# Seven quarter products for half of a feed-forward's first part, in idle score banks, and attention weights turned in place

## The chip, the cores and the metric

The kernel runs on one core of a Trainium2 chip. Its time is device time in microseconds (us); before the change it is 1347.37 us, the median of three runs (1346.15 to 1348.08). The engines are TensorE (PE in the profile; PEld is its weight loads), VectorE (DVE), ScalarE (ACT), GpSimd (POOL) and SyncE (SP, which only issues transfers here). Everything is float32.

## The reference

Attention with a threshold is followed by a normalised feed-forward block with a residual.

```python
# q, k, v: (8, 8, 576, 64): batch, heads, sequence, head size
scores = q @ k^T / 8
thresh = max(scores, -1) - tau                  # tau = 0.02
scores = where(scores >= thresh, scores, -1e9)
attn   = exp(scores - max) ; attn /= sum(attn) + 1e-9
x      = (attn @ v), heads side by side         # (8, 576, 512)
xn     = (x - mean) / sqrt(var + 1e-6) * g_ln
out    = x + relu(xn @ w_ch1) @ w_ch2           # w_ch1 512 x 2048, w_ch2 2048 x 512
```

## The kernel before

The main loop has 72 slots (`n`), nine for each of the 8 batches. A slot is one block of attention: two heads and half of the queries, or (the fifth of nine, `s == HP`) the last 32 queries of each half for all heads. In a slot

- PE computes the scores of the block into two PSUM areas, `sc[0]` and `sc[1]` (three banks each; the first 128 columns of each are free, `FREE`), named sc in the profile;
- DVE takes the row maxima (L419), ACT copies the finished values of an earlier block out (L621) and computes the exponentials into `e` (L432), DVE applies the threshold and sums the rows (L439, the masks), POOL divides (L455), and DVE turns `e` in 32 x 32 blocks into another tile, `et` (L529, or L523 for the fifth block); in between DVE turns new q and k (`turn`, L356 to L366) in slots that load them;
- SP stores `et` to a scratch tensor in DRAM (L540, scr<-et) and reloads it in the layout that PE needs (L554, em<-scr and L559, er<-scr);
- a slot later PE multiplies these turned weights by v (`values_of`, L598 sc<-em and L608 sc<-er, the value products), into the last columns of the score areas (`pv_behind`).

From slot 7 on all slots have one `e` tile, since `exponentials` picks `e_room[0]` for them.

The feed-forward works on 16 groups `g` of 288 tokens, two in each batch, numbered in the order in which they come ready. Its steps are a generator (`ffn_steps`), and `second_part` takes some of them in each of a slot's four quarters, by shares (`ROOM`): quarters 0 to 2 lie between the scores and the value products, quarter 3 between these and the rest of the value products (L608). So the order on every engine is fixed when the program is built, and each engine goes through its own list in order. A step that has no place in a quarter waits for the next one; nothing is put in its place while the chip runs.

- The first part (`first_part`) computes 16 tiles `p` of hidden units: four products of 128 x 128 weights with 288 tokens each, in one PSUM bank (two banks, `ps_ff`, are used in turn), and ACT's Relu (L796) takes each tile out. `product` splits each into two instructions of 64 columns of weights; a float32 instruction is two records in the profile. Beside it the variance is computed: Square on ACT (L802), three adds on POOL (L804), a product, three steps on ACT (L816 to L818), and `root` on DVE (L737 to L741).
- The second part (`second_quarters`, L101 seg in the profile) is already computed by seven quarter products in place of eight, with sums and differences by DVE and POOL (L872 and L912).

Where `drip`, `drops`, `aside` and `stores` appear, they are lists of small calls that are put among the rest of a slot.

Of the kernel before, what the change touches and what calls it, by code (L numbers as in the profile page):

```python
# [18 lines left out]
def kernel(  # L19
# [70 lines left out]
    hidden = consts.tile([128, ND, TOK], F32, name="hidden")  # L90
    e_room = [consts.tile([128, 4, S], F32, name=f"e{i}") for i in range(2)]

    units = [(b, hp) for b in range(B) for hp in range(HP)]
# [83 lines left out]
    class Weights:  # L177
# [13 lines left out]
        def __init__(self):  # L191
# [17 lines left out]
            self.raw, self.ticks = {}, 2  # L209
            flat = lambda t: t.rearrange("p a b -> p (a b)")  # L210

            x_room = ffn.tile([128, NK, TOK], F32, tag="x", bufs=3, name="x_room")
            y_room = ffn.tile([128, NK, TOK], F32, tag="sq", bufs=1, name="y_room")
            et_room = att.tile([128, NB, 128], F32, tag="et", bufs=1, name="et_room")
            stage = self.stage = consts.tile([128, 8, WC], F32, name="stage")
# [6 lines left out]
            for t, n, before in (  # L222
                (w2_sb.rearrange("p m d c -> p (m d) c"), ND // 2, lambda p: (16, 16, 19, 21, 24, 24, 25, 29)[p]),
                (hidden, 4, lambda p: 10),
                (x_room, 1, lambda p: 2 * n1),
                (y_room, 1, lambda p: 2 * n1),
                (et_room, 2, lambda p: n1 - 3),
                (stage, 4, lambda p: 2 * n1),
            ):
                for p in range(n):  # L230
                    home = 99 if t.shape[-1] != 128 or n != ND // 2 else n1 + 2 * p
                    self.free.append(
                        (before(p), -1, flat(t)[:, p * 2 * WC : (p + 1) * 2 * WC], home)
                    )
# [94 lines left out]
    FIRST = HP + 2  # L329

    def by_blocks(n):

        return n >= FIRST

    def scale_q(u, q_in):
# [75 lines left out]
    def exponentials(n):  # L411
# [17 lines left out]
        for i in range(4):  # L429
            if i == 2:  # L430
                yield es, thr
            nc.scalar.activation(es[:, i], blocks[i], func=AF.Exp, bias=neg[:, i : i + 1])  # L432

    def weights(es, thr, divide):


        den = small.tile([128, 4], F32, tag="den", name="den")
        for i in range(4):
            nc.vector.scalar_tensor_tensor(  # L439
                out=es[:, i], in0=blocks[i], scalar=thr[:, i : i + 1], in1=es[:, i],  # L440
                op0=ALU.is_ge, op1=ALU.mult, accum_out=den[:, i : i + 1],
            )
            if divide and i % 2:
                nc.vector.reciprocal(den[:, i - 1 : i + 1], den[:, i - 1 : i + 1])  # L444
# [3 lines left out]
        for i in range(4):  # L448
            if not divide:
                if i % 2 == 0:  # L450
                    two = ffn.tile([128, TOK], F32, tag="o", bufs=4, name="diag")
                diags.append(two[:, i % 2 * 128 : i % 2 * 128 + 128])
                nc.scalar.mul(diags[i], ident, den[:, i : i + 1])
                continue
            nc.gpsimd.tensor_scalar(  # L455
                out=es[:, i], in0=es[:, i], scalar1=den[:, i : i + 1], scalar2=1.0,
                op0=ALU.mult, op1=ALU.mult,
# [60 lines left out]
    def turn_blocks(b, s, es):  # L518


        et = att.tile([128, NB, 128], F32, tag="et", bufs=1, name="et")
        if s == HP:
            nc.vector.transpose(  # L523
                et.rearrange("p n (u c) -> p u n c", u=HP),
                es.rearrange("p u (n c) -> p u n c", c=32),
            )
        else:
            for h in range(2):
                nc.vector.transpose(  # L529
                    et[:, :, 64 * h : 64 * h + 64].rearrange("p n (j c) -> p j n c", j=2),  # L530
                    es[:, 2 * h : 2 * h + 2].rearrange("p j (n c) -> p j n c", c=32),
                )
        scr = dram.tile([4, S, 128], F32, tag="scr", name="scr")
        if b == 0:
# [219 lines left out]
    def differences():  # L754
# [9 lines left out]
        for eng, out, a, b, op in (  # L764
# [5 lines left out]
            for m in range(HM):  # L770
                for d in range(0, HD, 4):
                    at = (slice(None), m, slice(d, d + 4))
                    eng.tensor_tensor(out=out[at], in0=a[at], in1=b[at], op=op)
                    yield

    def first_part(g):

# [5 lines left out]
        for d in range(ND):  # L783
# [15 lines left out]
            if sq is None and d and (part > 1 or d == ND // 2 - 1):  # L799
                squared = d  # L800
                sq = hidden[:, ND - NK :]
                nc.scalar.activation(sq, xc, func=AF.Square)  # L802
                for c in range(1, NK):
                    nc.gpsimd.tensor_tensor(out=sq[:, 0], in0=sq[:, 0], in1=sq[:, c], op=ALU.add)  # L804
            elif sq is not None and rb is None and (
                d >= squared + (7 if plain else 3) and part > (0 if plain else 1)
                or d == ND - NK - 1
            ):
                var = ps_ff.tile([128, TOK], F32, tag="ff", name="var")
                product(var, lhsT=avg_sb, rhs=sq[:, 0], start=True, stop=True)  # L810
                rb = ffn.tile([128, TOK], F32, tag="rb", bufs=2, name="rb")
                two = [sq[:, c] for c in (2, 3)]
                if plain:
                    two = [ffn.tile([128, HM, HT], F32, tag="part", bufs=4, name="two") for _ in two]
                    two = [t.rearrange("p m t -> p (m t)") for t in two]
                nc.scalar.activation(two[0], var, func=AF.Identity, bias=eps_sb)  # L816
                nc.scalar.activation(rb, two[0], func=AF.Ln)
                nc.scalar.activation(rb, rb, func=AF.Exp, scale=-0.5)  # L818
                aside.append(lambda: root(rb, *two))
                yield 1, 1  # L820
# [21 lines left out]
    def second_quarters(g, rb):  # L842
# [68 lines left out]
        def add(eng, out, a, b):  # L911
            eng.tensor_tensor(out=out, in0=a, in1=b, op=ALU.add)  # L912

        def finish(eng, i, j=None):

# [52 lines left out]
        if not ends_here:  # L968
            later(
                ("12", 1, add, dve, y12, y12, p3), ("done12", 2, finish, pool, 0, 1),  # L970
                *((f"o{m}", 1, store, dve, g, m, y[:, m]) for m in (2, 3, 0, 1)),
            )
        yield 2, 0.5

    def ffn_steps(g):
        rb = yield from first_part(g)
        yield from (second_quarters if g else second_plain)(g, rb)

# [5 lines left out]
    ROOM = (0.6, 1.0, 1.25, 0.35)  # L984
    STEPS = [1 + NK * ND * 2] + [1 + NK * ND * 2 - NK * ND // 8] * (NG - 1)
    ends = [sum(STEPS[: i + 1]) for i in range(NG)]
# [19 lines left out]
    def second_part(n, i):  # L1006
# [11 lines left out]
        steps = 0  # L1018
        got = 1 if i in (0, QUARTERS - 1) else 2
        while queue and (owed >= 0.5 or got == 1 and i in (0, QUARTERS - 1)):  # L1020
            got, cost = next(queue[0], (None, 0))
# [6 lines left out]
            else:  # L1028
                issued += cost
                owed -= cost  # L1030
                steps += 1
                if steps == 4 and among:
                    mean_of(among[0])
                    centre(among.pop())

    def group_ready(g):
# [4 lines left out]
        else:  # L1041
            at_quarter(*before, mean_of, g)
            at_quarter(*(first if g and first[1] else before), centre, g)
        at_quarter(*first, lambda: queue.append(ffn_steps(g)))

# [43 lines left out]
    for n in range(NS):  # L1089
# [45 lines left out]
        blocks_go = by_blocks(n)  # L1135
        diags = weights(es, thr, blocks_go)
        run_all(aside)
# [9 lines left out]
        if blocks_go:  # L1147
            conversion.fetch(0 if n == FIRST + 2 else 3, wait=0)
            conversion.prepare_to(end_at, False)
            scr = turn_blocks(b, s, es)  # L1150
            if n == FIRST:
                conversion.take(e_room[1])
# [84 lines left out]
```

## Time and profile before

| what | value |
|---|---|
| median of the runs | 1347.37 us |
| span of the profiled execution | 1345.5 us |
| busy PE | 1313.5 us, 98% |
| busy DVE, POOL, ACT | 870.6, 621.9, 458.7 us (65%, 46%, 34%) |
| DMA, mean over the span | 159 GB/s |
| steady slots (from slot 18 on) | 15.4 to 19.9 us each, nine together 158.4 us |
| after the last scores (slot 71 starts 1231.9 us after the first instruction) | 113.6 us |

The median of the runs is taken outside the profiler; the span of the profiled execution, from its first to its last instruction, lies 1.9 us under the median. Busy time of matmuls counts each record, and the records overlap: a record of 288 columns lasts 408 ns by itself, but the next one starts after about 122. In a row of a group the columns are: line, engine, operation, output and inputs with their sizes, count, then busy time and mean duration, and last the idle time just before them with what ended it. In a timeline the columns are start and duration in us.

### The profile page before, as it was taken

The numbers are of one execution on the slowest core, as the hardware profiler recorded it, in microseconds if no ns is written. First come the engines' busy times: TensorE is split into PE (matmuls) and PEld (weight loads), VectorE is DVE, ScalarE is ACT, GpSimd is POOL, SyncE is SP. The second block draws the span as 40 slices with busy tenths as digits, with TensorE's granted clock in tenths as the row PEclk, the third lists the DMA queues.
The fourth block names the chain that finished last, engine by engine and source line by source line (L and its number), as shares of the span: only waits on it lengthen the run. The fifth ranks groups of instructions, "written<-read, shape, count | busy, mean of one in ns | idle before, by whom it ended". The sixth has DMA issues, their size and how long they took to land.

```text
span 1345.5 us, 40255 instructions
## 1 busy us (share of the span) xinstructions
PE 1313.5 (98%) x17304; PEld 989.7 (74%) x17304; DVE 870.6 (65%) x1544; ACT 458.7 (34%) x995; POOL 621.9 (46%) x836
## 2 busy tenths in 40 slices
PE   8898899999999999999999999999999999999997
PEld 7665567769686776868778696877869677786957
DVE  7879886667666675666756677656756667666112
ACT  5866333232323233232233324233232323333120
POOL 3475556534444444445535454443444445335312
PEclk9999999999999999999999999999999999999999
DMA  8937874557643775447734576447754476443211
GB/s 173 297 95 176 209 191 151 178 163 190 176 146 132 182 200 158 151 156 200 191 127 150 167 183 191 139 137 196 198 167 152 126 196 179 136 157 124 81 19 20
DMA packets 335298, 213.92 MB, mean 159 GB/s; under 512 B 247376, under 2 KB 292688, under 8 KB 327056
## 3 DMA queue, kind: packets, MB, share of 16 engines
q1 hardware_dynamic: 329008, 210.46, 54.6%
q8 instruction: 136, 2.23, 0.7%
q10 hardware_dynamic: 5952, 0.74, 0.4%
q0 software_dynamic: 160, 0.15, 0.1%
q14 instruction: 42, 0.34, 0.1%
HBM read 124.00 MB, written 87.29 MB: 157 GB/s over the span
## 4 chain that ended last, share of the span: by engine, by line
PE 91%; ACT 3%; DVE 2%; DMA 1%; POOL 1%; issue 1%; SPq 1%; POOLq 0%; ACTq 0%; DVEq 0%
PE p L101 38%; PE seg L101 31%; PE sc L405 10%; PE sc L598 9%; PE sc L608 2%; ACT e L432 1%; PE tp L101 1%; DVE e L439 1%; POOL w L308 1%; PE var L101 1%; PE mean L101 1%; SPq L118 0%; DMA scr<-et 0%; ACT em L489 0%; DMA k_in<-in_k_dram 0%
## 5 line engine op out<-in xcount | busy, mean ns | idle before, releaser
L101 PE MATMUL p<-xc,w 128*64 128x288 f32 x4096 | 517.1, 408 | 6.5 <-ACT part L887 4.6
L101 PEld LDWEIGHTS p<-xc,w 128*64 128x64 f32 x4096 | 287.7, 137 | 213.8 <-issue 13.5
L419 DVE TENSOR_REDUCE neg<-sc 128x2 f32<-128x1152 f32 x144 | 188.7, 1351 | 282.2 <-PE sc L405 281.6
L455 POOL TENSOR_SCALAR e<-e,den 128x576 f32<-128x576 f32 x264 | 205.9, 792 | 131.3 <-DVE den L444 131.3
L101 PE MATMUL seg<-hidden,w 128*64 128x144 f32 x3840 | 247.9, 287 | 0.0
L101 PEld LDWEIGHTS seg<-hidden,w 128*64 128x64 f32 x3840 | 234.9, 137 | 11.5 <-issue 8.5
L439 DVE SCALAR_TENSOR_TENSOR e<-sc,thr,e 128x576 f32<-128x576 f32 x288 | 222.4, 810 | 19.3 <-POOL thr L423 11.6
L423 POOL TENSOR_SCALAR thr<-neg,low_sb 128x2 f32<-128x2 f32 x144 | 39.4, 274 | 384.1 <-DVE neg L419 382.4
L796 ACT ACTIVATE hidden<-p 128x288 f32<-128x288 f32 x256 | 106.5, 416 | 305.3 <-PE p L101 303.7
L432 ACT ACTIVATE e<-sc,neg 128x576 f32<-128x576 f32 x288 | 197.6, 754 | 2.4 <-DVE neg L419 2.4
L529 DVE STREAM_TRANSPOSE et<-e 128x1152 f32<-128x1152 f32 x118 | 161.1, 1373 | 14.2 <-POOL e L455 13.7
L405 PE MATMUL sc<-kT,qT 64*64 64x384 f32 (+3 forms) x2048 | 140.3, 403 | 3.1 <-DVE e L439 3.1
L598 PE MATMUL sc<-em,v_in 128*64 128x128 f32 (+1 forms) x2368 | 130.9, 264 | 2.4 <-DVE w L293 2.4
L598 PEld LDWEIGHTS sc<-em,v_in 128*64 128x64 f32 x2368 | 124.0, 138 | 10.9 <-DVE w L293 2.6
L101 PE MATMUL seg<-hidden,stage 128*64 128x144 f32 x1920 | 123.3, 286 | 0.0
L101 PEld LDWEIGHTS seg<-hidden,stage 128*64 128x64 f32 x1920 | 117.6, 137 | 2.9 <-issue 2.9
L621 ACT COPY x<-sc 128x128 f32<-128x128 f32 x120 | 31.6, 265 | 245.2 <-PE sc L405 176.3
L405 PEld LDWEIGHTS sc<-kT,qT 64*64 64x64 f32 x2048 | 76.3, 133 | 44.6 <-issue 21.3
L872 POOL TENSOR_TENSOR hidden<-hidden 128x576 f32<-128x576 f32 x60 | 84.8, 1427 | 52.0 <-ACT hidden L796 42.4
L887 ACT COPY part<-seg 128x288 f32<-128x288 f32 x74 | 29.8, 403 | 190.6 <-PE seg L101 190.1
L872 DVE TENSOR_TENSOR hidden<-hidden 128x576 f32<-128x576 f32 x60 | 51.2, 887 | 51.5 <-PE seg L101 48.5
L101 PE MATMUL seg<-hidden,e 128*64 128x144 f32 x896 | 61.2, 286 | 0.0
(130 smaller groups left out, 1041.2 us busy)
## 6 DMA issues: line engine op xcount, KB each, us to landing
scr<-et SPq DMA_DIRECT2D x63, 1152.0 KB, 4.8
em<-scr SPq DMA_DIRECT2D x63, 1024.0 KB, 5.7
out_dram<-ot SPq DMA_DIRECT2D x248, 36.0 KB, 3.8
q_in<-in_q_dram SPq DMA_DIRECT2D x120, 72.0 KB, 2.7
er<-scr SPq DMA_DIRECT2D x132, 64.0 KB, 5.2
k_in<-in_k_dram SPq DMA_DIRECT2D x116, 72.0 KB, 3.0
v_in<-in_v_dram SPq DMA_DIRECT2D x28, 256.0 KB, 5.4
w<-in_moe_w_ch_dram SPq DMA_DIRECT2D x10, 512.0 KB, 7.0
```

Source lines behind the costliest of these rows:

```text
L101: nc.tensor.matmul(out[r], lhsT=lhsT[:, r], rhs=rhs, **flags)
L405: nc.tensor.matmul(sc[h][64 * i : 64 * i + 64, at : at + n], lhsT=ql[r] if s == HP else qT[r, half, j * 128 + 64 * i : j * 128 + 64 * i + 64],
L419: nc.vector.tensor_reduce(out=neg[:, i], in_=pairs[h], axis=AXL.X, op=ALU.max, negate=True,)
L423: nc.gpsimd.tensor_scalar(out=thr[:, i], in0=neg[:, i], scalar1=-1.0, scalar2=low_sb, op0=ALU.mult, op1=ALU.add,)
L432: nc.scalar.activation(es[:, i], blocks[i], func=AF.Exp, bias=neg[:, i : i + 1])
L439: nc.vector.scalar_tensor_tensor(out=es[:, i], in0=blocks[i], scalar=thr[:, i : i + 1], in1=es[:, i], op0=ALU.is_ge, op1=ALU.mult, accum_o ...
L455: nc.gpsimd.tensor_scalar(out=es[:, i], in0=es[:, i], scalar1=den[:, i : i + 1], scalar2=1.0, op0=ALU.mult, op1=ALU.mult,)
L529: nc.vector.transpose(et[:, :, 64 * h : 64 * h + 64].rearrange("p n (j c) -> p j n c", j=2), es[:, 2 * h : 2 * h + 2].rearrange("p j (n c) ...
L598: nc.tensor.matmul(dst[64 * h : 64 * h + 64], lhsT=vt[:, h, c, :], rhs=pick(em[:, 2 * j : 2 * j + 2, c], h), start=c == 0 and first, stop= ...
L621: nc.scalar.copy(x_of(2 * b + (s > HP))[:, s % (HP + 1), 128 * j : 128 * j + 128], pv[j])
L796: nc.scalar.activation(hidden[:, d], p1, func=AF.Relu)
L872: eng.tensor_tensor(out=out[at], in0=in0[at], in1=in1[at], op=op)
```

## The change

In the first part of groups 2 to 15, 8 of the 16 tiles are no longer computed one by one. They form two units of four tiles (0 to 3 and 12 to 15). A unit is a 2 x 2 block product: two halves of the hidden units, two halves of the input features, and two halves of the tokens (`early`, `late`), with seven products of quarters in place of eight. Five of the seven go into the banks of `ps_ff`, four of them one upon another in `chain`, which ACT copies out three times on the way; two go into the free first columns of the banks 0 and 1 of `sc[0]`, in the second half of a slot, after the masks have read the scores. DVE adds the parts (`sums_due`), and ACT takes the Relu in place.

The units need sums of the weights (`sums_of_w1`, made once during group 1) and of the tokens (`sum_x`, four subtractions in each group). The sums of weights lie in a new tile `extra`, with the last three pieces in `e_room[1]` and `ident`; up to slot 11 `extra` also serves as `et`, which is gone: from slot 12 on the weights of attention are turned within `e` itself, which for that is written in another order (`blocks_of`), and SP stores them from there. The variance of a group is computed after the first unit, and its Square at the start of that unit; before, both came at a count of tiles. A unit may start in a slot's third quarter of the slots in `unit_slots`, or as soon as no plain tile is left; a step that ends with 4 ends the quarter.

```diff
+    IN_PLACE = SLOTS + HP - 1
+    def blocks_of(es, i, n):
+        if n < IN_PLACE:
+            return es[:, i]
+        return flat(es).rearrange("p (n u c) -> p u n c", u=4, c=32)[:, i]
...
     def turn_blocks(b, s, es):
-        et = att.tile([128, NB, 128], F32, tag="et", bufs=1, name="et")
+        if b * SLOTS + s >= IN_PLACE:
+            et = flat(es).rearrange("p (n x) -> p n x", x=128)
+            for at in (slice(0, 128),) if s == HP else (slice(0, 64), slice(64, 128)):
+                nc.vector.transpose(et[:, :, at], et[:, :, at])
...
+    UNITS = (((0, 1), (2, 3)), ((12, 13), (14, 15)))
...
+    def sums_of_w1():
+        for k, (f1, f2) in enumerate(UNITS):
...
+                    for eng, out, a, b, op in (
+                        (nc.gpsimd, p3, a11, a21, ALU.subtract),
+                        (nc.vector, a21, a21, a22, ALU.add),
+                        (nc.vector, p2, a21, a11, ALU.subtract),
+                        (nc.gpsimd, p4, a12, p2, ALU.subtract),
+                    ):
+                        eng.tensor_tensor(out=out, in0=a, in1=b, op=op)
...
+    def sum_x(g):
+        while g - 1 not in last_added:
+            drops.pop(0)[-1]()
...
+        for eng, out, a, b in (
+            (nc.vector, t1, b12, b11), (nc.gpsimd, t3, b22, b12),
+            (nc.vector, t2, b22, t1), (nc.gpsimd, t4, b21, t2),
+        ):
+            eng.tensor_tensor(out=out, in0=a, in1=b, op=ALU.subtract)
...
+    def unit(g, xc, k):
...
+        chain = ps_ff.tile([128, 2, HT], F32, tag="ff", name="chain")
+        for _ in steps(chain, w_of(f1, 0), x_of(0, 0), True, False):
+            yield 3, 0.5
+        nc.scalar.copy(h12, chain)
+        p2 = ps_ff.tile([128, 2, HT], F32, tag="ff", name="p2")
+        for _ in steps(p2, w_of(f1, 1), x_of(1, 0), True, True):
+            yield 3, 0.5
+        add = lambda out, a, b: nc.vector.tensor_tensor(out=out, in0=a, in1=b, op=ALU.add)
+        sums_due.append(lambda: add(h11, p2, h12))
+        for end in steps(chain, s_of(0), t_of(t2), False, False):
+            yield 4 if end and part < 2 and now < QUARTERS * NS else 3, 0.5
+        nc.scalar.copy(h22, chain)
+        for _ in steps(other[0], w_of(f2, 0), t_of(t1), True, True):
+            yield 3, 0.5
+        sums_due.append(lambda: add(h12, other[0], h22))
+        for _ in steps(chain, s_of(1), t_of(t3), False, False):
+            yield 3, 0.5
+        nc.scalar.copy(h21, chain)
+        sums_due.append(lambda: add(h22, other[0], h21))
+        for end in steps(other[1], s_of(2), x_of(1, 1), True, True):
+            yield 4 if end and now < QUARTERS * NS else 3, 0.5
+        sums_due.append(lambda: add(h12, other[1], h12))
+        for end in steps(chain, w_of(f2, 1), t_of(t4), False, True):
+            if not end:
+                yield 3, 0.5
+        run_all(sums_due)
+        nc.scalar.activation(h21, chain, func=AF.Relu)
+        both = hidden[:, f1[0] : f1[0] + 2]
+        nc.scalar.activation(both, both, func=AF.Relu)
+        nc.scalar.activation(h22, h22, func=AF.Relu)
+        yield 2 if k else 3, 0.5
...
+    def first_units(g):
...
+            if k < len(UNITS) and (not plain or now // QUARTERS >= slots[k] and part > 1):
+                if g not in sums_of_x:
+                    sum_x(g)
+                if k == 0:
+                    squares(sq, xc)
+                yield from unit(g, xc, k)
+                k += 1
+                if k == 1:
+                    rb = variance(sq, [sq[:, c] for c in (2, 3)])
+                    yield 2, 1
+                continue
...
     def ffn_steps(g):
-        rb = yield from first_part(g)
-        yield from (second_quarters if g else second_plain)(g, rb)
+        rb = yield from (first_part if g < 2 else first_units)(g)
+        sums = sums_of_w1() if g == 1 else iter(())
+        for i, step in enumerate((second_quarters if g else second_plain)(g, rb)):
+            if i % 8 == 7:
+                next(sums, None)
+            yield step
...
-        got = 1 if i in (0, QUARTERS - 1) else 2
-        while queue and (owed >= 0.5 or got == 1 and i in (0, QUARTERS - 1)):
+        has_unit = g > 1 and n in unit_slots(g)
+        whole = i in (0, QUARTERS - 1) or i == 1 and has_unit
+        got = 1 if i in (0, QUARTERS - 1) else 3 if i == 2 and has_unit else 2
+        while queue and (owed >= 0.5 or got == 3 or got == 1 and whole):
...
+                if got == 4:
+                    break
...
             scr = turn_blocks(b, s, es)
+            run_all(sums_due)
```

## Prediction

> **What bounds the kernel now.** I read the page first (engines, then the costliest groups), then the trace slot by slot: the timeline of all engines for slots 16 to 21, then the windows. A slot is one pass of the main loop: scores of one block, its softmax, the value products of the block before, and a share of the feed-forward work.
>
> ```profile
> span 1345.5 us, 40255 instructions
> PE 1313.5 (98%) x17304; PEld 989.7 (74%) x17304; DVE 870.6 (65%) x1544; ACT 458.7 (34%) x995; POOL 621.9 (46%) x836
> ...
> L101 PE MATMUL p<-xc,w 128*64 128x288 f32 x4096 | 517.1, 408 | 6.5 <-ACT part L887 4.6
> ...
> L101 PE MATMUL seg<-hidden,w 128*64 128x144 f32 x3840 | 247.9, 287 | 0.0
> ```
>
> TensorE (PE) is busy 98%. The windows say where the other 2% lies: slots 16, 17 and 20 whole, then a stretch around a wait early in the run (columns: length, then busy time of PE, PEld, DVE, ACT, POOL, then the granted clock).
>
> ```profile
> 264.77:281.36 16.59, 16.57 (x181) 10.10 (x177) 11.61 (x21) 6.70 (x16) 7.75 (x10) 1.00 0.43 148
> 281.36:298.19 16.83, 16.83 (x192) 10.91 (x188) 10.14 (x18) 5.56 (x13) 6.94 (x10) 1.00 0.70 185
> 333.72:351.52 17.80, 17.80 (x193) 11.01 (x188) 11.56 (x22) 6.94 (x15) 10.07 (x13) 1.00 0.77 221
> 154.21:157.90 3.69, 3.69 (x30) 2.99 (x32) 3.59 (x8) 1.95 (x3) 3.69 (x5) 0.57 1.09 250
> ```
>
> In the steady slots PE has no gap at all: whatever PE does less is gained, and whatever it waits more is lost, one for one. The other engines are at 60% or less there, but each slot's softmax is one long chain. The timeline of slot 17 (start, duration):
>
> ```profile
> 283.40 11.38 PE L101 MATMUL p<-xc,w 128*64 128x288 f32 x92
> 283.51 2.62 DVE L419 TENSOR_REDUCE neg<-sc 128x2 f32<-128x1152 f32 x2 [4.14 <-PE sc L405]
> 285.06 1.38 ACT L432 ACTIVATE e<-sc,neg 128x576 f32<-128x576 f32 x2
> 286.32 0.42 ACT L796 ACTIVATE hidden<-p 128x288 f32<-128x288 f32 x1
> 286.61 1.39 ACT L432 ACTIVATE e<-sc,neg 128x576 f32<-128x576 f32 x2
> 291.42 1.38 DVE L529 STREAM_TRANSPOSE et<-e 128x1152 f32<-128x1152 f32 x1
> 293.07 1.38 DVE L529 STREAM_TRANSPOSE et<-e 128x1152 f32<-128x1152 f32 x1 [0.28 <-POOL e L455]
> 294.61 1.92 PE L598 MATMUL sc<-em,v_in 128*64 128x128 f32 x32
> ```
>
> From the end of the scores, VectorE (DVE) needs 283.51 to 294.45, 10.94 us, to the end of its second transpose; in slot 16 (no new q and k to turn) 9.45 us. The value products start at 294.61, but today they wait for neither transpose, only for the last mask (291.3): PE covers the chain with 11.2 us of first-part products.
>
> **The change, part by part.**
>
> *The saving.* A plain tile is 8 matmul instructions of 288 columns, two records each; a unit replaces 4 tiles (64 records) by 7 quarter products of 8 instructions (112 records of 144 columns, the shape of the seg rows). From stretches: 96 records p from 335.77 to the value products at 347.46 are 0.122 us each, and seg paces 0.0615 (80 records from 307.15 to 312.05). So a unit costs 6.9 us where 7.8 us were: 0.90 saved (by the busy times, 0.126 and 0.0646, 0.85). Two units in each of groups 2 to 15: 28 x 0.90 = 25 us.
>
> *The wait of the value products.* A quarter product (8 instructions) is 0.98 us. Two go to the score bank sc0, which the value products use next. In the program's order, in each unit slot, the first value product on sc0 now waits for the third sum on DVE (`h22 = other[0] + h21`), and that sum stands behind both transposes of the slot and behind the last quarter product in sc0. Behind that product on PE's queue stands everything else.
>
> Slot 16 (first unit): PE has 3 tiles and 6 quarter products, ending 14.0 us into the slot; DVE is through its transposes at 11.6. So two dependent sums are exposed (three dependent 288-wide operations of `root` took 1.41 us, 0.47 each), with 0.2 before and 0.07 after: 1.15, less the 0.1 that this passage costs today: 1.1. One more wait: `squares` puts its Square (1.16 us on ACT) ahead of the copy of the chain bank, which PE needs before it may go on accumulating there: 0.3. Together 1.4. Slot 20 (4 tiles): the same, 1.4.
>
> Slot 17 (second unit): only one tile is left, so PE has 1.95 + 6 x 0.98 = 7.8 us before the value products, where it had 11.2; DVE needs 10.94 and three sums, 1.41. Besides, `variance` now comes after the first unit, at the very end of slot 16. On ACT its three steps stand behind the unit's three Relus (0.4 + 0.75 + 0.4 + 0.5 + 0.44 + 0.44), so they end about 2 us into slot 17; `root` (1.41) is ahead of the new maximum on DVE, which starts at 3.5 us instead of 2.15. So: value products at 3.5 + 10.94 + 1.41 + 0.07 = 15.9 us; without waits at 2.05 + 7.8 + 0.1 = 10.0. Lost: 5.9 us. Inside that, the Relu of the tile and the chain copy queue behind late Exps on ACT (1.9 and 0.7), and the last gap is about 3.2.
>
> Slot 21 (second unit, two tiles, no turn): maximum again at 3.5; Relus behind the Exps hold PE 0.8 and 0.7; then as in slot 16, 1.1: 2.6 us.
>
> Sum: 7 batches hold a 16/17 pair, 1.4 + 5.9; 6 hold a 20/21 pair, 1.4 + 2.6 (group 15 runs after the last slot): 51.1 + 24.0 = 75 us.
>
> *Transposes in place.* The store of the turned weights (4.8 us median to landing, 2.5 to 7.5) now must land before the next slot's first Exp. The tightest steady slot is 19: transpose ends 330.67, first Exp of slot 20 at 337.43, and the reload that waits for the store went out at 336.26. So it is hidden, by 1.2 us. In slot 17 SP sends the store at 14.5 us instead of 13.1; with 4.8 it lands at 19.3, before the slot ends at 20, so neither the next Exp nor the reload behind it on SP is late. In slot 13 the one big transpose ended 1.0 us into slot 14, so Exp is late once: between 0 (PE's seg work covers it) and 2.6 us; I take 1. The strided forms of Exp, mask, scale and turn are not in the trace; the nearest rows are the transposes that already write 32-wide runs (1373 ns for 1152, 1.19 each, against 767 for 576 contiguous, 1.33): taken at no cost, bounds -10% and +10% of DVE's 10.94 us. Only slot 17, and 21 partly, would feel that: 7 us either way.
>
> *The rest.* `sum_x` adds 0.9 us on DVE before the maximum; in slot 20 DVE idles 1.91 there. If that were not free, 0.9 more in 6 slots. Sums of w1: 32 adds of 128 in slots 13 to 15, on engines with slack; if not hidden, at most about 0.3 each on either engine, 5 us. I take 0. Group 15 has no other work beside it: its copies are covered by the next quarter product, except the one behind Square: 0.5.
>
> Profiled execution: 1345.5 - 25 + 75 + 1.5 = 1397; the median lies 1.9 above its span, so 1399 us.
>
> **A rule against the change.** A long gap may cost more than itself, and the trace has one (the row from PE's own timeline):
>
> ```profile
> 154.21 1.75 PE L101 MATMUL p<-hidden,w 128*64 128x288 f32 x8 [4.07 <-POOL w L308]
> ```
>
> After these 4.07 us PE was granted a clock of 0.57 over the next 3.7 us, the last window above, which loses some 1.7 us; after an idle 2.35 us, up to 132.83, the next 4 us have a granted clock of 1.00. My last gap in slot 17 (3.2) lies between the two: 0 to 1.7 us in 7 slots, 0 to 12 us. I take 0, since the gap that did it was longer than any of mine.
> [...]
>
> **Rivals.**
> 1. *The waits are covered, the kernel is faster.* This holds if DVE is past its transposes before PE's last quarter product in every unit slot and the sums slip in unseen. Then 1347.4 - 25 + 2 = 1324. It decides when the loss per unit falls below 0.90 us; slot 17 would need its chain 5 us shorter. Against: slot 17's DVE rows above, and the order of sums on DVE. Chance 3%.
> 2. *`root` does not delay the maximum* (ACT is quicker through the Relus). Slots 17 and 21 lose 1.35 less: 13 x 1.35 = 18 us: 1381. For it: ACT is 34% busy; against: the last quarter product ends right before the scores. Chance 11%.
> 3. *The clock falls, or the strided forms cost more*, each by its bound above: 1411, 1406, both 1418. Chance 15%.
> 4. *The narrow products save nothing* (weight loads, 137 ns a record, become the limit): 1424. Against: seg rows with the same shape run gapless. 1%.
> 5. *The waits are as long as the saving: no change.* 1%.
>
> The forecast itself: 69%, its own range 1387 to 1409. The range 1379 to 1416 takes in rivals 2 and 3. Faster by over 0.2% (about what a measurement of this kernel can tell from none) is rival 1, 3%; within it 1%; slower 96%.
>
> **What would show it.** In the profile after: PE's busy time down by some 24 us, but its share of the span near 92%; first value products of slots 16 and 20 released by a DVE sum after about 1 us idle, in 17 after about 3; in slots 17 and 21 `root` directly ahead of the maximum, 1.3 us late; slot 17 about 20 us long. Wrong if PE stays at 98%, or if the gaps sit elsewhere (Exp waiting for the store).

## The result, and the profile after

The changed kernel takes **1424.95 us** (median of 4 runs, 1420.77 to 1426.84) against 1347.3: **1.0576 times the time before, 95% interval 1.0559 to 1.0593**, 78 us more. The prediction said slower with 0.96 and gave 1399 us with a range of 1379 to 1416, so the sign was right, and the size was 26 us short, 9 us outside the range.

The page of the kernel after, the lines that answer to those shown of before (the column after the bar: busy us, mean ns of one, then idle time just before the group and what ended it):

```profile
span 1423.4 us, 43420 instructions
PE 1313.2 (92%) x18648; PEld 1061.0 (75%) x18648; DVE 966.7 (68%) x1700; ACT 478.9 (34%) x1051; POOL 656.7 (46%) x880
...
L103 PE MATMUL p<-xc,w 128*64 128x288 f32 (+1 forms) x2752 | 326.7, 389 | 27.7 <-ACT hidden L956 21.3
...
L103 PE MATMUL seg<-hidden,w 128*64 128x144 f32 x3840 | 249.6, 288 | 6.6 <-DVE hidden L1049 3.7
...
L619 PE MATMUL sc<-em,v_in 128*64 128x128 f32 (+1 forms) x2368 | 137.7, 272 | 45.3 <-DVE hidden L888 43.5
```

PE is still busy for 1313 us, but only 92% of the span: it now idles 110 us instead of 32. The prediction had its busy time fall by some 24 us, and that sign did not come. An estimate from the two traces says why: stretches at half clock hold 28.9 us of PE's work (3.4 before), which makes some 13 us more, and there are 74 more gaps of over 0.1 us, ahead of each of which the last record counts in full, 0.17 us a time, another 13 us. Two groups carry most of the idle time. The value products (L619) waited 45.3 us, 43.5 of them for the unit's sums on DVE (L888), and the first-part products (`p`) 27.7, mostly for a Relu on ACT.

The windows of slots 34, 35 and 38, which are of the types of 16, 17 and 20, where the kernel before had lengths of 16.6, 16.8 and 17.8 and no gap, and a stretch in slot 14 (length; busy time of PE, PEld, DVE, ACT, POOL; granted clock; DMA):

```profile
613.40:632.30 18.90, 17.72 (x247) 13.49 (x242) 11.86 (x22) 7.12 (x16) 7.37 (x11) 1.00 0.39 131
632.30:652.80 20.50, 15.37 (x234) 12.32 (x230) 13.14 (x25) 7.70 (x18) 6.51 (x10) 1.00 0.64 167
688.10:710.60 22.50, 19.88 (x263) 14.56 (x259) 17.48 (x30) 7.58 (x17) 12.87 (x16) 1.00 0.63 169
240.80:244.20 3.40, 2.73 (x24) 2.76 (x26) 2.35 (x9) 2.09 (x5) 1.32 (x3) 0.50 0.89 319
```

Slot 17 type from the timeline (here slot 35, which begins at 632.3):

```profile
634.33 0.46 DVE L758 SCALAR_TENSOR_TENSOR hidden<-rb 128x288 f32<-128x288 f32 x1 [3.43 <-ACT rb L919]
...
635.69 2.61 DVE L431 TENSOR_REDUCE neg<-sc 128x2 f32<-128x1152 f32 x2
...
638.97 1.20 PE L103 MATMUL p<-xc,w 128*64 128x144 f32 x16 [1.49 <-ACT hidden L956]
...
640.52 1.20 PE L103 MATMUL chain<-t,extra 128*64 128x144 f32 x16 [0.35 <-ACT hidden L884]
...
642.88 1.15 PE L103 MATMUL chain<-t,extra 128*64 128x144 f32 x16
...
643.86 0.41 PE L103 MATMUL sc<-xc,extra 128*64 128x144 f32 x4
...
645.25 1.38 DVE L540 STREAM_TRANSPOSE e<-e 128x1152 f32<-128x1152 f32 x1 [0.28 <-POOL e L471]
646.55 0.42 DVE L888 TENSOR_TENSOR hidden<-p,hidden 128x288 f32<-128x288 f32 x1
647.10 1.02 DVE L888 TENSOR_TENSOR hidden<-sc,hidden 128x288 f32<-128x288 f32 x2
648.17 1.97 PE L619 MATMUL sc<-em,v_in 128*64 128x128 f32 x32 [3.17 <-DVE hidden L888]
```

This is the picture of the prediction nearly to the tenth: `root` ahead of the maximum, the second transpose ending 14.3 us into the slot, the sums behind it, the value products at 648.17, 15.9 us into the slot. Two starts, 642.88 and 643.86, also give the pace: a quarter product is 0.98 us.

Slot 20 type (slot 38, from 688.1) is what the prediction had not seen:

```profile
687.52 2.41 DVE L1089 TENSOR_TENSOR y<-y,part 128x288 f32<-128x288 f32 x3
...
689.69 1.50 POOL L1089 TENSOR_TENSOR y<-y,x 128x576 f32<-128x576 f32 x1
689.85 1.66 DVE L853 TENSOR_TENSOR t<-xc 128x288 f32<-128x288 f32 x1
691.15 1.01 POOL L853 TENSOR_TENSOR t<-xc 128x288 f32<-128x288 f32 x1
691.54 0.94 DVE L853 TENSOR_TENSOR t<-xc,t 128x288 f32<-128x288 f32 x1
692.41 2.61 DVE L431 TENSOR_REDUCE neg<-sc 128x2 f32<-128x1152 f32 x2
...
695.68 4.10 PE L103 MATMUL p<-xc,w 128*64 128x288 f32 x32 [1.44 <-ACT hidden L956]
...
706.95 1.97 PE L619 MATMUL sc<-em,v_in 128*64 128x128 f32 x32 [1.18 <-DVE hidden L888]
```

`sum_x` first forces the last additions of the group before (its `while` loop), and these hold DVE to 689.93. The first sum then begins on DVE just after an addition on POOL, and ends 0.32 us after that one, at 691.51 against 691.19. The two sums of `sum_x` that stand on DVE push the maximum from 690.3 to 692.4; the Exps and the Relu behind them on ACT follow, and PE waits 1.44 us for a bank that this Relu must empty, besides the wait of the value products that was foreseen.

Slots 13 and 14 (slot 14 begins at 230.2):

```profile
226.30 0.47 PE L103 MATMUL seg<-hidden,stage 128*64 128x144 f32 x4 [1.73 <-POOL hidden L1049]
...
228.06 0.29 DVE L833 TENSOR_TENSOR w<-w,w 128x128 f32<-128x128 f32 x1 [4.74 <-POOL extra L833]
...
232.76 2.57 DVE L540 STREAM_TRANSPOSE e<-e 128x2304 f32<-128x2304 f32 x1
...
235.25 2.58 DVE L431 TENSOR_REDUCE neg<-sc 128x2 f32<-128x1152 f32 x2
...
239.67 1.37 ACT L444 ACTIVATE e<-sc,neg 128x576 f32<-128x576 f32 x2 [2.80 <-DMA scr<-e]
...
241.47 5.44 PE L103 MATMUL seg<-hidden,w 128*64 128x144 f32 x64 [2.90 <-ACT part L1064]
249.26 0.71 PE L103 MATMUL seg<-hidden,w 128*64 128x144 f32 x8 [2.35 <-DVE hidden L1049]
```

The sums of w1 go back and forth between POOL and DVE, each waiting for the other; DVE stands 4.74 us in one of these waits with the big transpose of slot 13 behind it. The transpose starts 2.6 us into slot 14, the store of the turned weights goes out after it, the first Exp waits 2.80 us for that store, and PE in the end 2.90. PE waits twice more in these two slots, 1.73 and 2.35 us, for additions of the second part (L1049) on POOL and DVE that stood behind sums of w1.

Where the 78 us lie, by the lengths of slots (my sums from the two traces):

```
stretch          before     after     difference
slots 0 to 12     213.6     212.5        -1
slots 13 to 15     51.2      60.3        +9
slots 16 to 70    967.1    1035.2       +68  (6 batches x 9.6 + slot 70: 2.3 + half clock: 8)
from slot 71      113.6     115.4        +2
```

A batch of nine slots without half clock took 158.4 us before (slots 34 to 42) and takes 168.0 after. How much PE lost in each unit slot, measured by the starts of its records against their usual distance (0.122 us for a pair of 144 columns, 0.243 for a pair of 288), beside the prediction (for 16, 17, 20 and 21: slots 34, 35, 38 and 39):

```
slot      predicted   measured   of what
16           1.4         1.5      value products 1.35, short waits 0.16
17           5.9         6.0      p2 1.66, chain 0.52, first product in the score bank 0.30 (masks), value products 3.34, short waits 0.15
20           1.4         3.2      value products 1.35, p 1.66, short waits 0.16
21           2.6         2.7      chain (first product) 0.7, p2 0.5, value products 1.35, short waits 0.2
```

### The profile page after: what moved, and what is told of

Same layout as the page of the kernel before. It is cut to its first block, busy times and chain, and to the rows that moved or that the text cites. A ratio compares the mean times of both kernels' runs of the same rounds, so it can differ in the third digit from the quotient of the medians.

```text
span 1423.4 us, 43420 instructions
## 1 busy us (share of the span) xinstructions
PE 1313.2 (92%) x18648; PEld 1061.0 (75%) x18648; DVE 966.7 (68%) x1700; ACT 478.9 (34%) x1051; POOL 656.7 (46%) x880
## 5 line engine op out<-in xcount | busy, mean ns | idle before, releaser
L103 PE MATMUL p<-xc,w 128*64 128x288 f32 (+1 forms) x2752 | 326.7, 389 | 27.7 <-ACT hidden L956 21.3
L103 PEld LDWEIGHTS p<-xc,w 128*64 128x64 f32 x2752 | 187.9, 137 | 152.7 <-ACT hidden L956 27.8
L471 POOL TENSOR_SCALAR e<-e,den 128x576 f32<-128x576 f32 x264 | 198.9, 765 | 149.5 <-DVE den L459 149.4
L619 PE MATMUL sc<-em,v_in 128*64 128x128 f32 (+1 forms) x2368 | 137.7, 272 | 45.3 <-DVE hidden L888 43.5
L540 DVE STREAM_TRANSPOSE e<-e 128x1152 f32<-128x1152 f32 (+1 forms) x113 | 163.2, 1449 | 22.5 <-POOL e L471 22.4
L619 PEld LDWEIGHTS sc<-em,v_in 128*64 128x64 f32 x2368 | 126.2, 141 | 55.4 <-DVE hidden L888 50.4
L1049 POOL TENSOR_TENSOR hidden<-hidden 128x576 f32<-128x576 f32 x60 | 86.4, 1451 | 81.0 <-ACT hidden L910 57.2
L888 DVE TENSOR_TENSOR hidden<-sc,hidden 128x288 f32<-128x288 f32 x84 | 38.3, 458 | 75.0 <-PE sc L103 37.7
L956 ACT ACTIVATE hidden<-p 128x288 f32<-128x288 f32 x112 | 46.3, 421 | 93.5 <-PE p L103 93.5
L1049 DVE TENSOR_TENSOR hidden<-hidden 128x576 f32<-128x576 f32 x60 | 51.5, 893 | 29.6 <-PE seg L103 29.6
```

The source lines that it names most:

```text
L103: nc.tensor.matmul(out[r], lhsT=lhsT[:, r], rhs=rhs, **flags)
L471: nc.gpsimd.tensor_scalar(out=e, in0=e, scalar1=den[:, i : i + 1], scalar2=1.0, op0=ALU.mult, op1=ALU.mult,)
L540: nc.vector.transpose(et[:, :, at], et[:, :, at])
L619: nc.tensor.matmul(dst[64 * h : 64 * h + 64], lhsT=vt[:, h, c, :], rhs=pick(em[:, 2 * j : 2 * j + 2, c], h), start=c == 0 and first, stop= ...
L888: add = lambda out, a, b: nc.vector.tensor_tensor(out=out, in0=a, in1=b, op=ALU.add)
L956: nc.scalar.activation(hidden[:, d], p1, func=AF.Relu)
```

## The experiments

All are told as time, and as ratio to the kernel before run beside it (1346.5 to 1346.7 us).

**Turning in place alone** (`turn_alone`: the kernel before with `blocks_of`, `like` and the transposes within `e`, no units).

> The kernel before with the weights turned in place and nothing else: no units, no sums of weights or tokens; the first part as before. If the units' waits are the loss (my account now), this is 1347 to 1351: the in-place store only delays the first Exp of slot 14 by some 2.7 us, as the one big transpose of slot 13 ends late there. Rival: the strided forms and the wait of every Exp for the store are the larger part of the 78 us: 1390 or more.

1346.46 us, ratio 1.000 (0.999 to 1.0009). The strided forms and the store that must land before the next Exp cost no time by themselves: the first Exp of slot 14 comes later, 5.38 us into the slot instead of 3.71, but PE does not wait for it, and slots 13 to 15 take 51.2 us as before.

**No sums with the score bank** (`no_bank_sums`).

```diff
-        sums_due.append(lambda: add(h12, other[0], h22))
-        sums_due.append(lambda: add(h22, other[0], h21))
-        sums_due.append(lambda: add(h12, other[1], h12))
```

> The changed kernel without the three adds that read the score bank (h12 and h22 from other[0], h12 from other[1]); the hidden units of the eight tiles are therefore not complete. The value products then wait for the masks alone. My account: the gaps of 1.18 us in slots 16, 20, 21 and of 3.17 us in slot 17 go, 7 x 4.35 + 6 x 2.36 = 45 us, and with the long gap the half clock, some 8 us: 1425 - 53 = 1372 (1366 to 1382). Rival (the late maximum or the in-place store sets the slot, not the sums): under 15 us gained, 1410 or more.

1368.13 us, ratio 1.0159 (1.0143 to 1.0174): 57 us less. The wait for the bank is most of the loss, with the half clock that came with it: the mean granted clock is 0.995 in this run, 0.987 in the changed kernel. The run also takes three operations a unit off DVE; `covers` below keeps them, changes the order, and gains nearly as much.

**No `root`** (`no_root`: the kernel leaves it out in all groups but the first two).

> The changed kernel without root (the three steps on DVE that refine the inverse root) in groups 2 to 15. My account: the maximum of slots 17 and 21 starts at 2.15 instead of 3.5 us, worth 1.4 in slot 17 and 0.9 in slot 21: 7 x 1.4 + 6 x 0.9 = 15 us, and some of the half clock as the gap in slot 17 shortens to about 1.8: 1400 to 1411. Rival (root fills an idle DVE and delays nothing): 1422 to 1427.

1411.29 us, ratio 1.0478 (1.0462 to 1.0494): 13.7 us less. `root` ahead of the maximum is a term of its own, somewhat smaller than the 1.35 x 13 = 18 us of rival 2; half clock is left in this run, with a mean granted clock of 0.988 against 0.987 in the changed kernel (0.50 from 641.8 to 645.2).

**Sums of w1 in stages** (`w1_staged`: all of POOL's first subtractions are issued a step ahead of DVE's sums, these a step ahead of POOL's second ones; a stage comes at every sixth step in place of every eighth).

> The changed kernel with the sums of w1 issued in stages: POOL's difference of one piece, DVE's two steps of the piece before it, POOL's last step of the one before that, so that neither waits for the other; slots 13 to 15 only. My account: these slots lost 9.2 us because DVE waited for POOL piece by piece ahead of the big transpose; 4 to 8 us come back: 1417 to 1421. Rival (the late in-place store of slot 13 alone makes that loss): 0 to 2 us, 1423 to 1425.

1418.19 us, ratio 1.0531 (1.0515 to 1.0547): 6.8 us less. Slots 13 to 15 fell from 60.3 to 55.6 us. The 4 us over before that are left lie in slot 13 (19.59 us against 15.71): PE waits 1.99 us there for POOL's addition in `hidden` (L1053), and the mean granted clock is 0.97 over the 55.3 us from 213.0.

**Sums of x behind the masks** (`sum_x_later`).

```diff
-                at_quarter(first[0], 3 if first[1] else -1, sum_x, g)
+                at_quarter(first[0], 3 if first[1] else 2, sum_x, g)
```

> The changed kernel, but in the slots in which a group begins anew (20 and its like, six of them before the tail) the four sums of x, with the three additions forced ahead of them, are issued behind the masks instead of ahead of the maximum. Theory (they stand in front of the maximum on DVE and make the first-part products wait): the 1.66 us of stall between the records at 695.7 in slot 20 go, 6 x 1.66 = 10 us: 1415 us (1411 to 1418). Rival (what holds those products is the Exp or the Relu, whatever DVE does first, or the sums are now late for the unit): 1422 to 1428.

1427.27 us, ratio 1.0596 (1.0582 to 1.0611): no gain, the rival. The maximum came on time again (first Exp 3.70 us into slot 38 instead of 5.87), but a later row of that slot shows the wait that took its place:

```profile
706.58 0.79 POOL L853 TENSOR_TENSOR t<-xc 128x288 f32<-128x288 f32 x1
707.32 0.79 POOL L853 TENSOR_TENSOR t<-xc,t 128x288 f32<-128x288 f32 x1
707.42 1.20 PE L103 MATMUL chain<-t,extra 128*64 128x144 f32 x16 [1.89 <-POOL t L853]
```

POOL's two sums now stood behind its scaling and its products for the output, and the unit needs them.

**The same, all four sums on DVE** (`sum_x_dve`: `t3` and `t4` on DVE for groups that begin in slot 20).

> The changed kernel with the four sums of x of slot 20 behind the masks as in the run sum_x_later, but all four on DVE; there two were on POOL, came behind its scaling and products, and the unit's fifth product waited 1.89 us for them. Theory (the 1.66 us ahead of the maximum are a loss of their own, which the run before only moved to POOL): 6 x 1.66 = 10 us less than the changed kernel, 1415 us (1411 to 1419). Rival (the transposes and the sums of the unit, now later on DVE, take the gain back): 1421 to 1428.

1421.05 us (1414.53 to 1422.12), ratio 1.0542 (1.0522 to 1.0562). Slot 20 fell from 22.5 to 21.3 us, no `p` waits there any more, and beside the value products' 1.17 only 0.20 is left at the chain: 7 us over six slots. In the whole run about 4 are seen; the mean granted clock of the profiled execution is 0.986, against 0.987 in the changed kernel. So the rows of the slot show the mechanism, but it is worth 4 to 7 us, not 10. The total alone would not show it: it lies at the edge of the rival's range, and its interval touches that of the changed kernel.

**`root` behind the masks** (`root_later`: issued by `at_quarter(now // QUARTERS + 1, 1, ...)`).

> The changed kernel, root left in, but issued behind the masks of slots 17 and 21 instead of ahead of their maximum. Theory (root costs by its place, not by its work): as much as leaving it out gained, 13.7 us: 1411 us (1408 to 1416). Rival (it costs by DVE's time wherever it stands, since transposes and sums come behind it): 1419 to 1427.

1434.06 us, ratio 1.0647 (1.0633 to 1.0662): slower than the changed kernel, and above both expectations. In slot 35 of this run:

```profile
644.51 0.88 DVE L762 SCALAR_TENSOR_TENSOR rb<-hidden,rb 128x288 f32<-128x288 f32 x1
...
645.48 0.40 ACT L892 COPY hidden<-chain 128x288 f32<-128x288 f32 x1 [5.46 <-DVE rb L762]
645.93 1.95 PE L103 MATMUL chain<-t,extra 128*64 128x144 f32 x16 [3.33 <-ACT hidden L892]
```

The scratch of `root` is the last two tiles of `hidden`, which the second unit writes: its copy of the chain bank waits for `root`, and PE for the copy. Both theories had missed this use of one place by two steps.

**Two covers** (`covers`): the unit's last chain product goes ahead of the value products, and of these the ones of the other bank go first. (The unit's closing step also no longer counts in the shares: `yield 2 if k else 3, 0`.)

```diff
+        if not at_once:
+            order.sort(key=lambda x: -x[1][1])
...
-            yield 4 if end and now < QUARTERS * NS else 3, 0.5
+            yield 3, 0.5
         sums_due.append(lambda: add(h12, other[1], h12))
         for end in steps(chain, w_of(f2, 1), t_of(t4), False, True):
-            if not end:
-                yield 3, 0.5
+            yield 4 if end and now < QUARTERS * NS else 3, 0.5
```

> The changed kernel, but PE has 1.85 us of work between the unit's last product in a score bank and the value products that need that bank: the unit's last chain product (0.98) comes first, and of the value products those of the other bank (0.87). Theory (the wait is the sums on DVE, a fixed chain; and the half clock comes from a stretch of 3.41 us in which PE idles more than 2.0 us): the waits of 1.35 in slots 16, 20 and 21 go, that of 3.34 in slot 17 falls to 1.5, 39 us over the run, and no half clock is left in slots 17, 10 us more: 1376 us (1370 to 1384). Rival 1 (the half clock has another cause and stays): 1385 to 1390. Rival 2 (the value products then wait for something else as late): over 1400.

1370.4 us, ratio 1.0179 (1.0165 to 1.0193): 54.6 us less, at the lower end of the first theory. Slots 34, 35 and 38 of this run:

```profile
594.60:612.10 17.50, 17.50 (x244) 13.55 (x240) 11.77 (x22) 7.89 (x18) 7.39 (x11) 1.00 0.41 139
612.10:630.20 18.10, 15.10 (x228) 12.09 (x224) 13.06 (x25) 7.08 (x16) 7.71 (x10) 1.00 0.67 177
665.80:686.90 21.10, 19.66 (x264) 14.61 (x259) 17.37 (x30) 8.36 (x19) 12.86 (x16) 1.00 0.65 179
```

Slot 16 has no gap left, slot 17 three of 0.84, 0.35 and 0.13 at the unit's first products and one of 1.68 before the second half of the value products. The granted clock is 1.00 in all three windows and 0.995 in the mean of the run.

**All together, first attempt** (`all_five`: covers, sums of x behind the masks with two on POOL, `root` behind the masks, sums of w1 in stages, first sum ahead of the transposes).

> All together: sums of x behind the masks, root behind the masks, the two covers, the sums of w1 in stages, and the first sum of a unit ahead of the transposes on DVE. Theory (the terms add up): 1425 - 10 - 14 - 49 - 7 - 3 = 1342 us (1332 to 1352), so about as fast as the kernel before, the saving of 25 us being just eaten by what waits are left in slot 17. Rival (what one wait gives up the next takes back): 1355 to 1380.

1394.21 us, ratio 1.0355 (1.0341 to 1.037), above both expectations and worse than the covers alone: it holds the two moves that proved bad by themselves, and its slots 17 and 20 show the same 3.34 and 1.90 us at the chain.

**Covers, sums of x on DVE, sums of w1 in stages** (`covers_x`).

> The two covers (1370.4) with the sums of w1 in stages (6.8 less when done alone) and the sums of x behind the masks on DVE (10 less by theory). Theory: the terms add up where no wait of the same slot is left, 1353 us (1348 to 1359). Rival (a cover has already used the time): 1361 to 1368.

1358.17 us, ratio 1.0091 (1.0077 to 1.0104): the terms add up but for 5 us. 3 of these 5 lie in slots 13 to 15, which take 58.8 us where the stages alone left 55.6; in slot 14 PE waits 3.50 us there. Slot 20 is 19.7 us here (21.1 with covers alone): 8 us over six.

**Variance inside the first unit** (`best`, in all groups, with the sums ahead of the transposes in the second unit's slot; in the groups that begin in slot 20 the three adds of squares also go from POOL to DVE).

> As covers_x, and the variance taken inside the first unit, ahead of its last chain product, so that root follows the unit's sums on DVE and is over before the next slot's maximum; and in the second unit's slot the sums go ahead of the transposes, into the time in which DVE waits for the scaling. Theory (root ahead of the maximum and the late sums are what is left in slots 17 and 21, 3.7 us and 0.6 us a time): 1353 - 26 - 4 = 1323 us (1315 to 1336), faster than the kernel before by what the quarter products save. Rival (the transposes, now later, or the variance, now early, hold PE in their turn): 1340 to 1365.

1390.92 us, ratio 1.0325 (1.0302 to 1.0348), the rival and worse. Two rows of its timeline:

```profile
627.96 2.19 PE L103 MATMUL sc<-t,w 128*64 128x144 f32 x16 [1.68 <-DVE e L454]
...
716.97 1.37 ACT L444 ACTIVATE e<-sc,neg 128x576 f32<-128x576 f32 x2 [2.21 <-DMA scr<-e]
```

In slot 35 the unit came so early that its third product met the masks of its own slot; in slot 40 the first Exp was held by the store of weights that had been turned late in slot 39. So the in-place turn, free alone, sets a limit as soon as something delays the transposes enough: here they end 15.16 us after the start of slot 39, in `covers_x` 12.19. Which of the moves cost how much was not taken apart.

**The same in slots 16 and 17 alone, one plain tile moved** (`best2`).

```diff
+        if k == 0 and g % 2 == 0:
+            sums_due.pop(0)()
+            rb = variance(sq, [sq[:, c] for c in (2, 3)])
+            yield 3, 1
...
+            if g % 2 == 0 and len(plain) <= 2 and now // QUARTERS == slots[0]:
+                yield 0, 0
+                continue
...
+            if in_second[0]:
+                run_all(sums_due)
             scr = turn_blocks(b, s, es)
```

> As covers_x, but in the groups whose units stand in slots 16 and 17 alone: the variance inside the first unit (root then follows the unit's sums, ahead of no maximum), one plain tile moved from slot 16 to slot 17, and in slot 17 the sums ahead of the transposes. In the run best the same was done in slots 20 and 21 too, and there the late transposes held the store of the weights and with it the Exp of slot 22 (2.21 us), and in slot 17 the unit came so early that it waited for the masks (1.69). Theory (with these two causes taken away the 3 to 3.7 us of slot 17 are gained): 1358 - 7 x 3.3 = 1335 us (1327 to 1345), faster than the kernel before. Rival (the new order in slots 16 and 17 has waits of its own): 1348 to 1365.

**1343.3 us** (1340.66 to 1344.45), **ratio 0.997 (0.9958 to 0.9982)**: a little faster than the kernel before. Its page, then its windows of slots 34, 35 and 38:

```profile
span 1342.7 us, 43372 instructions
PE 1298.2 (97%) x18648; PEld 1054.8 (79%) x18648; DVE 958.4 (71%) x1714; ACT 481.5 (36%) x1051; POOL 651.3 (49%) x866
```

```profile
586.10:602.40 16.30, 15.90 (x228) 12.30 (x222) 11.37 (x21) 8.63 (x19) 7.39 (x11) 1.00 0.39 134
602.40:619.40 17.00, 16.90 (x252) 13.86 (x248) 13.37 (x27) 6.19 (x14) 7.72 (x10) 1.00 0.55 129
654.50:674.20 19.70, 19.50 (x260) 14.70 (x256) 15.33 (x30) 8.45 (x19) 11.92 (x14) 1.00 0.69 191
```

Its batch is 157.0 us, 1.5 less than before, where four units save 3.6; the rest are short waits, 0.3 to 0.5 us at the chain in each unit and 0.4 before the variance. 7 us over before still lie in slots 13 to 15.

## Why the prediction was right, and where it was wrong

- *The saving, 25 us: right by the pace.* 0.98 us a quarter product, 6.9 us a unit, as the `seg` rows had said. No run shows the whole saving free of waits; the nearest, `best2`, gains 1.5 us of 3.6 in a batch.
- *The waits of the value products and of `p2`, 75 us: right in mechanism and nearly in size.* Per slot 1.5, 6.0 and 2.7 against 1.4, 5.9 and 2.6. They are causal: without the sums that read the bank 57 us go, with 1.85 us of cover 54.6, without `root` 13.7. Rival 2 (`root` not late) did not come. For slot 20 the 1.4 holds for the value products only. That slot 16 agrees so well is in part luck: the 0.3 for the chain copy behind Square did not come (no gap stands at the chain there), and the value products waited 1.35 where 1.1 was forecast.
- *`sum_x` "adds 0.9 us on DVE before the maximum; in slot 20 DVE idles 1.91 there": the first step that failed.* Taken 0, bound 5; measured 1.66 x 6 = 10 us. The forced additions of the group before had used up the idle time, and beside POOL the first subtraction took 1.66 us and the second 0.94, where the estimate had 0.45 for each. It was a cost hidden by a gap that the change itself fills. Taken out of that place, 7 us of it are gained in the slots.
- *Sums of w1 and the Exp of slot 14, 1 + 0: the second step that failed.* Slots 13 to 15 are 9 us longer. The prediction had the right wait (the first Exp for the in-place store) but priced it with the transpose where it had been. "Engines with slack" did not help: the sums depend on each other across two engines, and DVE stood in them with the transpose behind it. And it had no term for what the sums of w1 put off on POOL and DVE themselves. The trace has the 9 us nearly whole: 2.90 for the late Exp, 1.73 and 2.35 for the second part's additions, and 1.3 for a half-speed stretch at 240.8 (2.69 us of PE's work in it). In stages, 5 of these 9 us went.
- *Half clock, 0, bound 12: the third.* In six stretches of 3.41 us between slot 16 and its last product PE ran at 0.5, with 19.4 us of its work in them. Over all stretches at 0.50 of this trace a pair of records of 144 columns starts every 0.241 us, at full clock every 0.123. So an estimated 9.7 us are lost, 8 of them up to slot 70, which is what the batches differ by. The prediction took zero because the one gap seen had been longer than its own. Its two rows could not tell the length of a gap from its place: of the 2.35 us before 132.83, after which the clock stayed at 1.00, 2.02 lie in one window of the grid described below, of the 4.07 us before 154.21 2.92.
- *Strided forms and the store, 0: right*, by `turn_alone`.

The three failed steps are 10 + 8 + 10 = 28 us of the 26 that were missing (slots 0 to 12 gave 1 back). Each had been taken at or near its lower end, 0 or 1, with a bound of 5, 7 and 12 us more noted beside it: 1399 with these three bounds is 1423. Two of the three came out above their bounds, 10 against 5 and 8 against 7. The range had let them come only one at a time.

## What to carry to other kernels

A cost that is "hidden" is hidden by a certain piece of idle time in a certain slot: look whether the change puts something else into it, and if several terms are set to zero by that argument, let the range take their bounds together. A product that writes into a bank which the next step on the same queue needs is only as cheap as the sums that empty the bank; order the queue so that work on other banks stands between (here two moves of order, 1.85 us a time, were worth 55 us). Before a step is moved out of the way, list who shares its scratch and what stands behind it on the next engine: two of the moves here (`sum_x_later`, `root_later`) were lost to that.

## What the runs showed of the hardware

*Where the half clock stood.* In the trace of the changed kernel the nine starts of clock 0.50, the first at 131.53 and the last at 1418.35, lie whole numbers of times 3.4133 us apart, to 0.001 us. Seven of these stretches last 3.41 us, the one at 476.27 twice as long (6.83), and the last runs past the end. The kernel before has two, at 154.70 and 1342.54, 348 times this length apart to 0.01 us. Steps of this length, counted on and back from these starts, make a grid that divides each of the two traces into windows. Two slots of one type with the same gap of 3.17 us, each with the window up to a point of the grid and the one behind it, in the changed kernel:

```profile
305.60:309.00 3.40, 1.36 (x24) 1.36 (x26) 1.75 (x4) 0.00 (x0) 0.45 (x1) 1.00 0.80 275
309.00:312.40 3.40, 3.40 (x34) 3.40 (x32) 0.46 (x1) 0.40 (x2) 0.00 (x0) 0.50 0.77 192
643.55:646.96 3.41, 1.46 (x24) 1.19 (x20) 3.13 (x4) 0.40 (x1) 2.84 (x4) 1.00 0.58 90
646.96:650.37 3.41, 2.20 (x40) 2.20 (x42) 1.32 (x4) 0.00 (x0) 0.00 (x0) 1.00 0.91 303
```

With 1.36 us of work in the window the next ran at half speed, with 1.46 it did not. The seven long gaps of slots 17 in the changed kernel:

```
gap of PE            most idle time in one window of the grid    next window
304.47 to 307.64     2.03                                        half
474.19 to 477.36     2.09, then 1.09 at half speed               half, half again
645.01 to 648.17     1.93                                        full
813.04 to 816.21     2.01                                        full
981.28 to 984.45     3.00                                        half
1150.99 to 1154.15   2.04                                        half
1320.43 to 1322.45   2.02                                        half
```

In the two traces, from 20 us after the start on, all nine windows at full clock with 2.021 us or more of idle time were followed by half clock, and none with less than 1.832. Of the six between, two were (1.832 and 1.989) and four were not (1.837, 1.933, 2.014 and 2.016). Six of the seven gaps are 3.17 us long, and what lies of them in one window differs by their place: 1.93 to 3.00. A batch of the changed kernel takes 49.2 windows (168.0 us), so the place shifts from one to the next. In the run without `root` a window of 3.40 us, from 638.4, had 3.17 idle, and 0.50 followed in the 3.40 behind it. Single runs of the changed kernel differ by 6 us where the kernel before differs by 2; this would fit, but one trace of the kernel doesn't show it. In `covers`, whose longest gap in slots 34, 35 and 38 is 1.68 us, the clock is 1.00 in all three.

*DVE beside POOL.* In the changed kernel all 26 operations of `sum_x` that DVE ran beside POOL ended 0.31 or 0.32 us after the POOL operation that had begun before them. A subtraction of 288 columns took 0.46 us on DVE in `sum_x_later` (at 701.85), and 1.66 in the changed kernel, where it had been started 0.16 us after a POOL operation of 1.50 and ended 0.32 after it (rows 689.69 and 689.85). The two of the last group, which had no POOL operation beside them, took 0.41 and 0.46 (at 1361.36 and 1361.81). A step of `root` took 0.46 ahead of the maximum (at 634.33), and two of the three took 0.88 beside POOL's scaling in `root_later` (at 643.59 and 644.51). What makes these ends follow POOL's is not shown: no run here was made to try it by itself. One pair of rows of `sum_x_later` goes the other way:

```profile
701.67 2.08 POOL L471 TENSOR_SCALAR e<-e,den 128x576 f32<-128x576 f32 x2 [0.19 <-DVE den L459]
701.85 0.46 DVE L853 TENSOR_TENSOR t<-xc 128x288 f32<-128x288 f32 x1
```

DVE ran at full pace although POOL's record begins 0.18 us earlier. But POOL's two scalings took 2.08 us there, where the two before them took 1.46 (at 700.02), so it may be POOL that waited; that is not shown.
